# Loading the first 2 MiB of a weight in eight DMAs of 16 strided partitions instead of one of 128

## The chip, the cores and the metric

One core of a Trainium2 chip runs the whole program. The metric is the device time of one execution in microseconds (us). The profile's span of the same execution is about 2 us shorter. The kernel before lay between 139.34 and 139.55 us in six runs.

## The reference

A decode step of a transformer block for 4 tokens, in bf16: layer norm, attention over a window of the last 2048 cached keys, and a gated feed-forward part, with two residual additions.

```python
x = A_x                                                    # [4, 1, 1024]
h  = x + attention(layernorm(x), k_cache, v_cache, wq, wo)   # 32 heads of 128, 4 kv heads
h2 = h + (silu(n @ w1) * (n @ w3)) @ w2                      # n = layernorm(h), F = 3584
```

With 4 tokens there is little arithmetic for each byte. About 55.6 MB of weights and cache have to be read once; wq alone is 8.4 MB.

## The kernel before

All big loads go through one plan. Each takes a 32 KB-a-partition buffer (`stream`, five of them) and is issued on the sync queue, in order, as buffers come free. The first load of wq is cut in two pieces of 2 MiB, so that the q matmuls can begin when the first has landed.

```python
wq_v = A_wq.rearrange("(p i) n -> p (i n)", i=KC)     # 128 partitions, 64 KB each

def load_rows(src, n, r0, pieces):
    t = stream.tile([P, SLOT], BF16, tag="s")
    i = 0
    for m in pieces:
        nc.sync.dma_start(
            out=t[:, i * n : (i + m) * n], in_=src[:, (r0 + i) * n : (r0 + i + m) * n]
        )
        i += m
    return [t[:, k * n : (k + 1) * n] for k in range(i)]
# ... (load_k, load_v alike)
plan = (
    [("wq", load_rows, (wq_v, N_Q, c, [2, 2] if c == 0 else [4])) for c in range(0, KC, RQ)]
    + [("k", load_k, (b,)) for b in range(0, B, BS)]
    # ... v, wo, w1, w3, w2
)
# ...
nc.scalar.dma_start(out=x_sb[:], in_=x_flat)
load_next(5)
# ...
for j in range(JG):          # x once more in another layout; first used after the attention
    nc.scalar.dma_start(
        out=x_q[QD * j : QD * (j + 1) : RS, :], in_=x_flat[:, j * CG : (j + 1) * CG]
    )
# ... layer norm, transposes of x
for kc in range(KC):         # q = x wq, one matmul group for each 1 MiB of wq
    ...
```

Of the kernel before, what the change touches and what calls it, by code (L numbers as in the profile page):

```python
# [10 lines left out]
P = 128  # L11
# [8 lines left out]
def kernel(  # L20
# [13 lines left out]
    nc = tc.nc  # L34

    B, _, D = A_x.shape
    Hkv, Sk, Dh = A_k_cache.shape[1], A_k_cache.shape[2], A_k_cache.shape[3]
    Hq = A_wq.shape[1] // Dh
    REP = Hq // Hkv
    W = min(4096, max(256, Sk // 4))  # L40
    F = B_w1.shape[1]
    KC = D // P
    FC = F // P
    NK = W // P
    NSB = W // 512
    assert B == 4 and D == KC * P and F == FC * P and Hq * Dh == 4096
    assert Dh == P and W == NK * P and B * Hq == P and Hkv == 4
    eps = 1e-5
    qscale = float(Dh) ** -0.5
# [42 lines left out]
    def load_rows(src, n, r0, pieces):  # L92

        t = stream.tile([P, SLOT], BF16, tag="s")
        i = 0
        for m in pieces:
            nc.sync.dma_start(  # L97
                out=t[:, i * n : (i + m) * n], in_=src[:, (r0 + i) * n : (r0 + i + m) * n]
            )
            i += m  # L100
        return [t[:, k * n : (k + 1) * n] for k in range(i)]

# [13 lines left out]
    def load_v(b):  # L116
# [11 lines left out]
    N_Q, N_F = Hq * Dh, F  # L128
# [3 lines that stand above are left out]
        + [("v", load_v, (b,)) for b in range(0, B, BS)]  # L132
        + [("wo", load_rows, (wo_v, D, c, [RO])) for c in range(0, IO, RO)]
        + [("w1", load_rows, (w1_v, N_F, c, [RQ])) for c in range(0, KC, RQ)]
        + [("w3", load_rows, (w3_v, N_F, c, [RQ])) for c in range(0, KC, RQ)]
        + [("w2", load_rows, (w2_v, D, 0, [16])), ("w2", load_rows, (w2_v, D, 16, [5, 4, 2, 1]))]
    )
    loaded = {}
    cursor = [0]
# [19 lines left out]
    for j in range(JG):  # L159
        nc.scalar.dma_start(  # L160
            out=x_q[QD * j : QD * (j + 1) : RS, :], in_=x_flat[:, j * CG : (j + 1) * CG]
# [7 lines left out]
    for c in range(2):  # L169
# [8 lines left out]
        out=xn[:], in0=x_sb[:], scalar1=mv[:, 0:1], scalar2=rstd[:, 0:1],  # L178
# [4 lines left out]
    for kc in range(KC):  # L183
# [15 lines left out]
        out=perm[:].rearrange("p (h dq) -> p h dq", dq=JG),  # L199
        in_=ident[:].rearrange("p (dq h) -> p h dq", dq=JG),  # L200
# [7 lines left out]
    for j in range(2, JG):  # L208
        nc.vector.tensor_tensor(
            out=same[:, 0, :], in0=same[:, 0, :], in1=ident[:, j * QD : (j + 1) * QD], op=ALU.add  # L210
# [24 lines left out]
    for r in range(REP):  # L235
        nc.tensor.transpose(out=qt_ps[:, r, :], in_=q_sb[:, r * Dh : (r + 1) * Dh], identity=ident[:])  # L236
    nc.vector.tensor_copy(
        out=qz[:, :, : Hkv * QD].rearrange("p b (g z) -> p b g z", g=Hkv)[:, :, :, :REP],
        in_=qt_ps[:].rearrange("p r (g x) -> p x g r", g=Hkv)[:, :B, :, :],
# [24 lines left out]
    for u, (b, n) in enumerate(units):  # L264
        k_v = loaded["k"][b].rearrange("p (j d) -> p j d", d=Dh)
        kT = ktpool.tile([P, NJ, P], BF16, tag="kT")
        for t in range(NJ // TB):
            kt_ps = psA.tile([P, TB, P], BF16, tag=f"kt{nt % 4}")
            for jj in range(TB):
                nc.tensor.transpose(  # L270
                    out=kt_ps[:, jj, :], in_=k_v[:, n * NJ + t * TB + jj, :], identity=ident[:]
# [23 lines left out]
        out=Pm[:].rearrange("q (c jq) -> q jq c", jq=NSB), in_=scores_ps[:].rearrange("q (jq c) -> q jq c", jq=NSB),  # L295
# [51 lines left out]
    for i in range(IO):  # L347
# [33 lines left out]
        out=hn[:], in0=h1[:], scalar1=tot[:, 0:1], scalar2=rstd2[:, 0:1],  # L381
# [5 lines left out]
        out=hnT[:].rearrange("p k x -> p (k x)"), in_=hn[:].rearrange("q (c k) -> q k c", k=KC)  # L387
# [5 lines left out]
    def gate_up(kind, out_ps):  # L393
# [27 lines left out]
        out=hgT[:].rearrange("p i x -> p (i x)"),  # L421
        in_=hg[:].rearrange("q s c -> q (s c)").rearrange("q (c i) -> q i c", i=IF),
# [47 lines left out]
```

## Time and profile before

| | before |
|---|---|
| median of 6 runs (lowest to highest) | 139.42 us (139.34 to 139.55) |
| DMA engines busy from, to (profiled run, span 137.4) | 1.77 us, 133.18 us |
| one 16 KB packet of the first 2 MiB, median after the first 16 | 0.611 us |
| first q matmul on wq | 8.20 us |

First come lines of the kernel before's page: the two lines of the 40 slices that concern the DMA engines (busy share in tenths; GB/s moved), the packet count, and the chain of work that ended last, by engine and by line.

```profile
DMA  5999999999999999999999999999999999998950
GB/s 155 444 402 520 391 391 444 420 429 444 405 440 392 421 421 414 423 495 476 401 391 424 453 428 397 459 467 401 409 459 439 426 409 430 448 458 359 420 217 2
DMA packets 4773, 55.74 MB, mean 406 GB/s; under 512 B 376, under 2 KB 408, under 8 KB 2716
...
DMA 70%; PE 19%; ACT 6%; SPq 1%; DVE 1%; issue 1%; ACTq 0%
```

From the second slice to the third last the 16 DMA engines are at 90% or more, but for one slice at 80 to 90%. The kernel is one long load with arithmetic beside it. The chain is 70% DMA.

The windows of the first microseconds of the kernel before follow. The columns are the stretch and its length, busy us (and count) of PE, PEld, DVE, ACT and POOL, the granted TensorE clock, the DMA share and the GB/s. A packet is counted whole in the window in which it starts, so a share can pass 1.

```profile
2.00:4.00 2.00, 0.00 (x0) 0.00 (x0) 1.76 (x5) 0.11 (x1) 0.15 (x1) 1.00 0.77 303
4.00:6.00 2.00, 0.00 (x0) 0.00 (x0) 0.45 (x2) 1.47 (x2) 0.00 (x0) 1.00 0.95 402
6.00:8.00 2.00, 0.65 (x8) 0.65 (x9) 1.44 (x9) 0.00 (x0) 0.00 (x0) 1.00 1.01 428
8.00:10.00 2.00, 1.80 (x16) 0.50 (x16) 0.31 (x3) 0.00 (x0) 0.00 (x0) 1.00 1.07 460
10.00:12.00 2.00, 0.08 (x4) 0.00 (x0) 0.00 (x0) 0.00 (x0) 0.00 (x0) 1.00 1.00 418
12.00:14.00 2.00, 1.05 (x12) 0.38 (x15) 0.00 (x0) 0.00 (x0) 0.00 (x0) 1.00 1.22 524
```

In the windows from 4 us on the stream runs at 400 GB/s and more. The kernel before's timeline (start, length, engine, line, operation) gives the issue of the three wq DMAs, first, on the sync queue:

```profile
0.73 1.33 SPq L97 DMA_DIRECT2D t<-in_A_wq_dram  x3
```

and, on PE, the first matmuls that need them, with the wait just before:

```profile
8.20 1.88 PE L222 MATMUL q_ps<-t,xnT 128*4 128x512 bf16 x16 [1.26 <-DMA t<-in_A_wq_dram]
```

And these are the three long waits of its chain that ended last (start, length, what):

```profile
1.63 20.98 DMA t<-in_A_wq_dram
...
54.23 36.88 DMA t<-in_B_w_dram
...
95.17 37.81 DMA t<-in_B_w_dram
```

The chain goes through a load three times: for wq at the start, and for two stretches of 37 us in the feed-forward part. Between them compute sets buffers free, but the DMA queue has work all that time, so an early loss in the stream reaches the end.

A note on packets. A packet is the piece in which the trace records what a DMA moves: the first 2 MiB stand there as 128 packets of 16 KB, as many as there are partitions with a row of 16 KB. In the trace of before 16 packets are under way at once for 116 of the 137 us. The trace records the start, the length and the size of each packet. It doesn't say which engine or which DMA it was; slices are told apart by the order of their packets, an average over the engines is a sum divided by 16, and numbers "from the packet records" below are counted from these records.

### The profile page before, as it was taken

The numbers are of one execution on the slowest core, as the hardware profiler recorded it, in microseconds if no ns is written. First come the engines' busy times: TensorE is split into PE (matmuls) and PEld (weight loads), VectorE is DVE, ScalarE is ACT, GpSimd is POOL, SyncE is SP. The second block draws the span as 40 slices with busy tenths as digits, with TensorE's granted clock in tenths as the row PEclk, the third lists the DMA queues.
The fourth block names the chain that finished last, engine by engine and source line by source line (L and its number), as shares of the span: only waits on it lengthen the run. The fifth ranks groups of instructions, "written<-read, shape, count | busy, mean of one in ns | idle before, by whom it ended". The sixth has DMA issues, their size and how long they took to land.

```text
span 137.4 us, 2307 instructions
## 1 busy us (share of the span) xinstructions
PE 71.2 (52%) x1045; PEld 45.2 (33%) x1045; DVE 36.3 (26%) x63; ACT 29.0 (21%) x28; POOL 1.6 (1%) x7
## 2 busy tenths in 40 slices
PE   0152304798989889100995579544090530802960
PEld 0110001175656565000894457221030210302830
DVE  6430000244444444601400300530003970160001
ACT  0400000155564646098610000000005000000000
POOL 4000000000000000000000000000000000000000
PEclk9999999999999999975555555558655586555555
DMA  5999999999999999999999999999999999998950
GB/s 155 444 402 520 391 391 444 420 429 444 405 440 392 421 421 414 423 495 476 401 391 424 453 428 397 459 467 401 409 459 439 426 409 430 448 458 359 420 217 2
DMA packets 4773, 55.74 MB, mean 406 GB/s; under 512 B 376, under 2 KB 408, under 8 KB 2716
## 3 DMA queue, kind: packets, MB, share of 16 engines
q1 hardware_dynamic: 4724, 55.58, 95.4%
q8 instruction: 8, 0.13, 0.3%
q10 hardware_dynamic: 40, 0.02, 0.0%
q14 instruction: 1, 0.01, 0.0%
HBM read 55.59 MB, written 0.01 MB: 405 GB/s over the span
## 4 chain that ended last, share of the span: by engine, by line
DMA 70%; PE 19%; ACT 6%; SPq 1%; DVE 1%; issue 1%; ACTq 0%
DMA t<-in_B_w_dram 54%; DMA t<-in_A_wq_dram 15%; PE kt_ps L270 9%; ACT kT L276 5%; PE scores_ps L255 5%; PE q_ps L222 3%; PE g_ps L398 2%; SPq L97 1%; PE y_ps L428 1%; DVE q_sb L232 1%; ACT q_sb L233 0%; DVE res L438 0%; PE qt_ps L236 0%; ACTq L276 0%
## 5 line engine op out<-in xcount | busy, mean ns | idle before, releaser
L276 ACT COPY kT<-kt_ps 128x1024 bf16<-128x1024 bf16 x16 | 15.8, 1014 | 12.0 <-PE kt_ps L270 12.0
L270 PE MATMUL kt_ps<-ident,t 128*128 128x128 bf16 x256 | 16.5, 219 | 0.0
L270 PEld LDWEIGHTS <-t 128*128 128x128 bf16 x256 | 14.4, 98 | 5.0 <-issue 4.9
L274 DVE COPY kT<-kt_ps 128x1024 bf16<-128x1024 bf16 x16 | 11.1, 692 | 15.2 <-PE kt_ps L270 15.2
L398 PEld LDWEIGHTS <-hnT 128*32 128x32 bf16 x128 | 5.5, 140 | 25.0 <-issue 22.7
L222 PE MATMUL q_ps<-t,xnT 128*4 128x512 bf16 x64 | 7.2, 615 | 12.0 <-DMA t<-in_A_wq_dram 12.0
L398 PE MATMUL u_ps<-t,hnT 128*32 128x448 bf16 x64 | 6.4, 576 | 10.6 <-DMA t<-in_B_w_dram 10.6
L255 PE MATMUL scores_ps<-kT,qz 128*32 128x512 bf16 x64 | 9.9, 609 | 3.1 <-ACT kT L276 3.1
L428 PE MATMUL y_ps<-t,hgT 128*32 128x256 bf16 x112 | 6.7, 415 | 7.6 <-DMA t<-in_B_w_dram 7.6
L398 PE MATMUL g_ps<-t,hnT 128*32 128x448 bf16 x64 | 6.3, 574 | 8.0 <-DMA t<-in_B_w_dram 8.0
L322 PE MATMUL OT_ps<-PT_sb,t 128*128 128x8 bf16 x256 | 7.4, 168 | 1.9 <-issue 1.7
L428 PEld LDWEIGHTS <-hgT 128*32 128x32 bf16 x112 | 4.8, 139 | 10.0 <-issue 5.5
L349 PE MATMUL y_ps<-t,o 128*32 128x256 bf16 x128 | 7.2, 418 | 1.7 <-DMA t<-in_A_wo_dram 0.9
L322 PEld LDWEIGHTS <-t 128*128 128x128 bf16 x256 | 7.3, 104 | 2.1 <-issue 2.0
L222 PEld LDWEIGHTS <-xnT 128*4 128x4 bf16 x64 | 2.0, 111 | 16.4 <-issue 16.1
L308 PE MATMUL pt_ps<-Dm,Pm 128*128 128x128 bf16 x16 | 1.9, 308 | 9.3 <-DVE Dm L301 9.3
L349 PEld LDWEIGHTS <-o 128*32 128x32 bf16 x128 | 5.1, 144 | 3.5 <-issue 1.2
L412 DVE RECIPROCAL eg<-eg 128x896 f32<-128x896 f32 x1 | 5.8, 5754 | 0.0
L232 DVE TENSOR_SCALAR q_sb<-q_ps 128x512 bf16<-128x512 f32 x1 | 0.7, 692 | 17.8 <-PE q_ps L222 17.8
L233 ACT ACTIVATE q_sb<-q_ps 128x512 bf16<-128x512 f32 x1 | 0.6, 597 | 21.4 <-DVE q_sb L232 21.4
L308 PEld LDWEIGHTS <-Pm 128*128 128x128 bf16 x16 | 1.6, 142 | 9.8 <-ACT Pm L294 9.8
L294 ACT ACTIVATE Pm<-scores_ps,nmax 128x2048 bf16<-128x2048 f32 x1 | 4.8, 4783 | 0.0
(67 smaller groups left out, 37.0 us busy)
## 6 DMA issues: line engine op xcount, KB each, us to landing
t<-in_B_w_dram SPq DMA_DIRECT2D x4, 3584.0 KB
t<-in_A_k_cache_dram SPq DMA_DIRECT2D x4, 2048.0 KB, 25.6
t<-in_A_v_cache_dram SPq DMA_DIRECT2D x4, 2048.0 KB, 33.0
t<-in_A_wo_dram SPq DMA_DIRECT2D x2, 4096.0 KB, 32.5
t<-in_A_wq_dram SPq DMA_DIRECT2D x2, 2048.0 KB, 9.6
t<-in_A_wq_dram SPq DMA_DIRECT2D x1, 4096.0 KB, 21.0
t<-in_B_w_dram SPq DMA_DIRECT2D x1, 4096.0 KB, 39.9
t<-in_B_w_dram SPq DMA_DIRECT2D x1, 1280.0 KB, 34.9
```

Of the source, the lines that this page charges most:

```text
L222: nc.tensor.matmul(q_ps[QD * g : QD * g + B, hf * 512 : (hf + 1) * 512], lhsT=xnT[:, kc, :], rhs=wq_t[:, c0 : c0 + 512], start=(kc == 0), ...
L255: nc.tensor.matmul(scores_ps[QD * g : QD * (g + 1), n * 512 : (n + 1) * 512], lhsT=qz[:, b, g * QD : (g + 1) * QD], rhs=kT_v[:, g, :, :], ...
L270: nc.tensor.transpose(out=kt_ps[:, jj, :], in_=k_v[:, n * NJ + t * TB + jj, :], identity=ident[:])
L274: nc.vector.tensor_copy(out=kT[:, t * TB : (t + 1) * TB, :], in_=kt_ps[:])
L276: nc.scalar.copy(out=kT[:, t * TB : (t + 1) * TB, :], in_=kt_ps[:])
L294: nc.scalar.activation(out=Pm[:].rearrange("q (c jq) -> q jq c", jq=NSB), in_=scores_ps[:].rearrange("q (jq c) -> q jq c", jq=NSB), func=A ...
L308: nc.tensor.matmul(pt_ps[:, jj, :], lhsT=Pm[:, (jb * JPB + jj) * P : (jb * JPB + jj + 1) * P], rhs=Dm[:], start=True, stop=True)
L322: nc.tensor.matmul(OT_ps[:, b, g * REP : (g + 1) * REP], lhsT=v_t[:, g, j, :], rhs=PT_sb[:, j, g * QD + b * REP : g * QD + (b + 1) * REP], ...
L349: nc.tensor.matmul(y_ps[QD * j : QD * (j + 1), :], lhsT=o4[:, i, :, :].rearrange("p b s -> p (b s)"), rhs=loaded["wo"][i][:, j * CG : (j + ...
L398: nc.tensor.matmul(out_ps[QD * j : QD * (j + 1), hf, :HF], lhsT=hnT[:, k, :], rhs=loaded[kind][k][:, c0 : c0 + HF], start=(k == 0), stop=( ...
L412: nc.vector.reciprocal(out=eg[:], in_=eg[:])
L428: nc.tensor.matmul(y2_ps[QD * j : QD * (j + 1), :], lhsT=hgT[:, i, :], rhs=loaded["w2"][i][:, j * CG : (j + 1) * CG], start=False, stop=(i ...
```

## The change

The intent is to have all 16 DMA engines start at once. With one DMA of 128 partitions the first 16 packets start one after the other over 0.44 us (1.77 to 2.21 us in the trace of before). Each of the eight DMAs of 16 partitions has 16 packets. The rows of one DMA are 8 partitions apart.

```diff
-            nc.sync.dma_start(
-                out=t[:, i * n : (i + m) * n], in_=src[:, (r0 + i) * n : (r0 + i + m) * n]
-            )
+
+            step = 8 if cursor[0] == 0 and i == 0 else 1
+            for p0 in range(step):
+                nc.sync.dma_start(
+                    out=t[p0:P:step, i * n : (i + m) * n],
+                    in_=src[p0:P:step, (r0 + i) * n : (r0 + i + m) * n],
+                )
             i += m
```

An unused constant (`FC`) goes too; that compiles to nothing. Below, one of the eight DMAs is called a slice.

More of the change, by code (lines that the diff above doesn't have):

```diff
@@ L42 @@
     KC = D // P
-    FC = F // P
     NK = W // P
     NSB = W // 512
-    assert B == 4 and D == KC * P and F == FC * P and Hq * Dh == 4096
+    assert B == 4 and D == KC * P and F % P == 0 and Hq * Dh == 4096
     assert Dh == P and W == NK * P and B * Hq == P and Hkv == 4
```

## The prediction

> **What bounds the kernel now.** The loads. The page counts 55.7 MB at a mean of 406 GB/s, and its line of DMA shares is at 9 (90% or more) in nearly every slice. Windows of 2 us show no gap: the 16 DMA engines are busy from 1.63 us, when the first packet of wq starts, to about 133 us; a tail of 4 us follows. The chain that ended last is 70% DMA; PE is busy 52% of the span. When the first w1 load is issued at 54.2 us, 33.5 MB had been asked for and about 22 MB delivered (estimate from the windows), so the queue doesn't run dry. The time is start of the stream + its service time + tail; what the change does to the stream moves the end one for one.
>
> **The start now.** The first DMA of 2 MiB is issued at 0.73 us (0.4 us). Its first 16 packets, 16 KB each, start between 1.63 and 2.1 us and end at 2.7 to 3.2 us, however early they started. After that a 16 KB packet takes 0.61 us on every engine (packet records of the trace). The last of 8 per engine ends at 7.5 us; the first q matmul starts at 8.20 us.
>
> **What the change does.**
> 1. It removes the stagger of the first packets: 0.1 to 0.3 us less, as their ends hardly depend on their starts.
> 2. It adds seven issues of about 0.4 us, 2.9 us on the sync queue. An issue is shorter than a packet (0.61 us), so the engines stay fed. Some later issues will wait for reused semaphores; none should starve the engines. Seven more completion packets of 9 ns per engine: 0.1 us.
> 3. It changes which partitions are written together. [...] No run here shows this yet.
> So I expect a 16 KB packet of these DMAs to take about 1.2 us instead of 0.61: 8 x 0.6 = +4.9 us on the stream.
>
> **Sum.** -0.2 + 0.1 + 4.9 = +4.8 us, nearly all on the critical path: 144.2 us; I say 144.0. [...] Range 139.1 to 144.8. Chances: faster by over 2%: 0.01; within 2%: 0.29; slower by over 2%: 0.70.
>
> **What would show it.** Right: between 2 and 12 us the windows' GB/s fall to about 210 while the DMA share stays near 1; the packets take 1.2 us; the first q matmul starts at about 13 us; everything later is shifted by nearly 5 us, its stages unchanged. Wrong: packets stay at 0.61 us and the first matmul starts at about 8 us.
>
> **What would make it wrong.** [...] Or an issue costs more than 0.6 us and starves the engines: then gaps show between 2 and 8 us.

The 1.2 us, twice the measured 0.61 us, was the assumption. The three terms of the sum, -0.2, +0.1 and +4.9, come to +4.8 us, and 139.4 + 4.8 is 144.2 us. The outcome without the long packets: the first two terms alone, 139.3 us or a little less.

What 1 and 2 rest on is in the packet records of before: the first packet to start (1.77 us) ends at 3.00 us, the last of the first 16 to start (2.21 us) at 3.02 us, and a completion packet has a median length of 9 ns.

The times that it takes from the packet records (1.63, 2.7 to 3.2, 7.5 us) are counted from an origin about 0.13 us late. On the profile's axis the first packet starts at 1.77 us and the last of the first 2 MiB ends at 7.65 us. The differences that it sums are not touched by this.

## The result, and the profile after

| | before | after |
|---|---|---|
| median of 6 runs (lowest to highest) | 139.42 us (139.34 to 139.55) | 145.0 us (144.16 to 145.88) |
| ratio, 95% interval | | 1.040 (1.0345 to 1.0456) |
| first packet starts | 1.77 us | 2.14 us |
| one 16 KB packet of the first 2 MiB, median after the first 16 | 0.611 us | 1.220 us |
| last packet of the first 2 MiB ends | 7.65 us | 12.10 us |
| last big packet ends | 133.18 us | 137.94 us |

A ratio is the mean time of one kernel's fast runs over that of the other's fast runs of the same rounds, so it is not quite the ratio of the medians. The trace of after is of its fastest run (144.16 us, span 142.2). The six runs scatter over 1.7 us, those of before over 0.2.

The same lines of after's page:

```profile
DMA  5998999999999999999999999999999999998950
GB/s 141 224 221 300 447 443 433 396 420 443 438 438 391 416 421 422 416 423 527 443 406 410 424 408 459 408 444 436 411 444 432 420 436 486 415 424 365 424 229 2
DMA packets 4885, 55.74 MB, mean 392 GB/s; under 512 B 488, under 2 KB 520, under 8 KB 2828
...
DMA 69%; PE 19%; ACT 5%; ACTq 2%; SPq 1%; issue 1%; DVE 1%
```

The second to fourth slice fell to between 221 and 300 GB/s while the busy share stayed at 8 to 9. From there on the lines look as they did. There are 112 packets more, the completion packets of seven more DMAs (16 each).

The same windows of the kernel after:

```profile
2.00:4.00 2.00, 0.00 (x0) 0.00 (x0) 1.76 (x5) 0.00 (x0) 0.15 (x1) 1.00 1.13 279
4.00:6.00 2.00, 0.00 (x0) 0.00 (x0) 0.24 (x2) 1.58 (x2) 0.00 (x0) 1.00 1.11 231
6.00:8.00 2.00, 0.64 (x8) 0.56 (x8) 1.48 (x8) 0.00 (x0) 0.00 (x0) 1.00 1.03 232
8.00:10.00 2.00, 0.00 (x0) 0.00 (x0) 0.47 (x4) 0.00 (x0) 0.00 (x0) 1.00 0.81 180
10.00:12.00 2.00, 0.00 (x0) 0.00 (x0) 0.00 (x0) 0.00 (x0) 0.00 (x0) 1.00 1.10 246
12.00:14.00 2.00, 0.79 (x8) 0.27 (x12) 0.00 (x0) 0.00 (x0) 0.00 (x0) 1.00 0.88 360
```

About 230 GB/s with the engines busy. They work nearly all the time and move half as much. The window from 8 to 10 us is emptier (0.81): by the packet records only 9 of 16 engines have a packet under way at 9.1 us, between the sixth and the seventh slice.

The issue of the ten wq DMAs, in the timeline of after's sync queue:

```profile
0.73 9.34 SPq L99 DMA_DIRECT2D t<-in_A_wq_dram  x10
```

The first matmuls on wq, in its timeline of PE:

```profile
13.21 1.88 PE L225 MATMUL q_ps<-t,xnT 128*4 128x512 bf16 x16 [6.07 <-DMA t<-in_A_wq_dram]
```

And the three long waits of its chain that ended last, with two pieces just before the first of them:

```profile
2.82 5.62 DMA x_q<-in_A_x_dram
8.45 0.53 SPq L99
...
9.66 18.04 DMA t<-in_A_wq_dram
...
59.45 36.34 DMA t<-in_B_w_dram
...
99.89 37.84 DMA t<-in_B_w_dram
```

The first matmul on wq comes 5.0 us later (13.21 against 8.20). The two late waits for the feed-forward weights begin 5.2 and 4.7 us later, and they are as long as before (36.34 and 36.88, 37.84 and 37.81 us). So nearly all of the loss is made in the first 12 us and carried to the end. New in the chain is an x_q load of 2 KB, 5.62 us long, after which an issue of wq follows. Before, the chain began with the wq issues themselves.

The ten wq issues took the sync queue 9.34 us instead of 1.33 for three. Its own waits in the first 16 us show why (who, for what, us in total, times, longest). In the kernel before no wq issue waits; the three longest waits are of the k and v loads:

```profile
SPq L121 <- PE kt_ps L270: 27.2, 1, 27.2
SPq L109 <- DMA t<-in_A_wq_dram: 5.2, 1, 5.2
SPq L121 <- DMA t<-in_A_wq_dram: 1.7, 1, 1.7
```

After the change wq's own issues (L99) wait:

```profile
SPq L99 <- DMA x_q<-in_A_x_dram: 2.3, 2, 1.7
SPq L99 <- DMA t<-in_A_wq_dram: 1.3, 1, 1.3
```

In the records of the issues each DMA names a semaphore by which it tells that it has landed, called its completion semaphore here. The program has eight of them (100, 102 to 106, 108, 110) and reuses them in turn; an issue that reuses one waits for it. In the trace of after the fourth slice and those after it reuse one. The fifth, for one, has the semaphore of the first slice, whose 16 signals come from 3.67 to 4.53 us, and is issued at 4.55 us, 1.3 us after the issue of the fourth ended. Three of the slices have semaphores of the tiny x_q loads (2 KB each). These are not needed until after the attention, but here a slice isn't issued before they land: the seventh waits 1.7 us, until 7.84 us. What it costs, e8 shows.

### The profile page after: what moved, and what is told of

Read it like the earlier page. It is cut to its first block, busy times and chain, and to the rows that moved or that the text cites. A ratio compares the mean times of both kernels' runs of the same rounds, so it can differ in the third digit from the quotient of the medians.

```text
span 142.2 us, 2317 instructions
## 1 busy us (share of the span) xinstructions
PE 68.9 (48%) x1045; PEld 43.6 (31%) x1045; DVE 36.3 (26%) x63; ACT 29.0 (20%) x28; POOL 1.6 (1%) x7
## 4 chain that ended last, share of the span: by engine, by line
DMA 69%; PE 19%; ACT 5%; ACTq 2%; SPq 1%; issue 1%; DVE 1%
DMA t<-in_B_w_dram 52%; DMA t<-in_A_wq_dram 13%; PE kt_ps L273 8%; ACT kT L279 5%; PE scores_ps L258 5%; DMA x_q<-in_A_x_dram 4%; PE q_ps L225 3%; PE g_ps L401 2%; SPq L99 1%; ACTq L163 1%; PE y_ps L431 1%; DVE q_sb L235 0%; ACT q_sb L236 0%; ACTq L152 0%; DVE res L441 0%
## 5 line engine op out<-in xcount | busy, mean ns | idle before, releaser
L431 PE MATMUL y_ps<-t,hgT 128*32 128x256 bf16 x112 | 5.8, 371 | 8.7 <-DMA t<-in_B_w_dram 8.7
L431 PEld LDWEIGHTS <-hgT 128*32 128x32 bf16 x112 | 4.3, 128 | 10.6 <-issue 6.3
L352 PE MATMUL y_ps<-t,o 128*32 128x256 bf16 x128 | 6.4, 394 | 0.8 <-DVE o L341 0.8
```

The costliest lines, as they stand in the source:

```text
L352: nc.tensor.matmul(y_ps[QD * j : QD * (j + 1), :], lhsT=o4[:, i, :, :].rearrange("p b s -> p (b s)"), rhs=loaded["wo"][i][:, j * CG : (j + ...
L431: nc.tensor.matmul(y2_ps[QD * j : QD * (j + 1), :], lhsT=hgT[:, i, :], rhs=loaded["w2"][i][:, j * CG : (j + 1) * CG], start=False, stop=(i ...
```

## The experiments

There were twelve experiments, in four groups on one chip each, every group with the kernel before beside it (139.38 to 139.45 us in the median). SBUF is the on-chip memory whose 128 partitions the loads fill. Theory A says that what counts is which partitions a slice writes: that packets to some sets of them take longer. In some expectations, times and packet lengths that stand without a name are theory A's (for e12 see there). Its rivals are that reads 512 KB apart are slow (the pitch), and that small DMAs cost by their number.

| run | first 2 MiB as | median us (range) | ratio | packet, median |
|---|---|---|---|---|
| e1 | the change again | 144.92 (144.22 to 145.62) | 1.041 | 1.18 |
| e7 | the change's partitions, neighbouring HBM rows | 145.53 (144.45 to 146.16) | 1.043 | 1.22 |
| e3 | 8 x 16 neighbouring partitions | 151.19 (150.51 to 151.5) | 1.083 | 2.13 |
| e6 | 8 x 16 partitions, step 4, halves | 144.52 (143.93 to 145.76) | 1.037 | 1.12 |
| e4 | the change's slices, alternating | 143.62 (143.39 to 144.92), three fast runs | 1.033 | 1.05 |
| e12 | 4 x 32 partitions, step 4 | 140.5 (140.31 to 140.84) | 1.007 | 0.61 |
| e2 | 8 x 128 partitions of 2 KB | 142.0 (141.22 to 142.08) | 1.018 | (2 KB) |
| e9 | e2 with x_q moved | 141.52 (141.38 to 141.6) | 1.015 | (2 KB) |
| e5 | the change (x_q not really moved) | 145.64 (144.18 to 145.96) | 1.043 | 1.25 |
| e8 | the change with x_q moved | 143.92 (143.75 to 144.0) | 1.032 | 1.27 |
| e11 | e8 again | 143.91 (143.86 to 144.13) | 1.033 | 1.27 |
| e10 | the kernel before with x_q moved | 139.15 (138.97 to 139.22) | 0.998 | 0.62 |

The last column is the median length of a 16 KB packet of the first 2 MiB, without the first 16, in us.

### e1: the change again

The edit: none.

> The changed kernel itself, again. Its six runs fell into two groups, 144.2 to 144.3 us and 145.7 to 145.9 us, and only one of the first group left a trace. All theories expect the two groups again. Theory 'late slice' (the seventh slice's issue waits for the semaphore of an x_q load, which lands late behind long wq packets): in a trace of the second group the gap of the DMA engines between the sixth and the seventh slice is about 1.5 us longer than in the first trace (0.5 us there). Rival[...]: in the second group the 16 KB packets of the first 2 MiB take longer, with a mean near 1.4 us instead of 1.2, and no longer gap.

144.22 to 145.62 us, four runs. The "two groups" were an accident of six runs, since 144.57 and 145.28 lie between them. So what is there is a scatter of 1.7 us. The traced run (144.57) is of neither group, so the two theories were not tested as stated; its packets took 1.18 us, not the 1.4 of the rival. See "The scatter" below.

### e7: same partitions, other rows

```diff
-                    out=t[p0:P:step, ...], in_=src[p0:P:step, ...],
+                    out=t[q:P:8, ...], in_=src[16 * q : 16 * q + 16, ...],
```

A small copy permutes x to match, so the result is right.

> The changed kernel writes the same partitions (p0, p0+8, ...) in each of the eight DMAs, but reads 16 neighbouring rows of wq for them (64 KB apart instead of 512 KB), with x permuted to match, so the result stays right. [...] as the changed kernel, 144.0 to 146 us, packets of about 1.2 us. Rival 'HBM pitch' (reads 512 KB apart are slow): packets of about 0.61 us, 139.4 to 140.2 us.

145.53 us, packets of 1.22 us. The pitch of the reads is out: with rows 64 KB apart the slices are as slow as with 512 KB. What e7 keeps from the change is where the slices write.

### e3: 16 neighbouring partitions

```diff
-            for p0 in range(step):                 # step = 8 for the first piece
-                nc.sync.dma_start(out=t[p0:P:step, ...], in_=src[p0:P:step, ...])
+            for a in range(8):                     # first piece only
+                nc.sync.dma_start(out=t[16*a : 16*a+16, ...], in_=src[16*a : 16*a+16, ...])
```

> Eight DMAs of 16 neighbouring partitions each[...]. [...] packets of the first 2 MiB take about 2.4 us, the stream is 8 x 1.8 = 14.6 us longer than before: 153 to 155 us. Rival (any DMA of 16 partitions costs the same, however they lie): 144 to 146 us, packets of 1.2 us.

151.19 us, packets of 2.13 us. Three windows of e3:

```profile
6.00:8.00 2.00, 0.65 (x8) 0.57 (x8) 1.43 (x9) 0.00 (x0) 0.00 (x0) 1.00 0.90 108
8.00:10.00 2.00, 0.00 (x0) 0.00 (x0) 0.32 (x3) 0.00 (x0) 0.00 (x0) 1.00 0.90 108
10.00:12.00 2.00, 0.00 (x0) 0.00 (x0) 0.00 (x0) 0.00 (x0) 0.00 (x0) 1.00 0.96 115
```

The engines are 90% busy or more and move 108 to 115 GB/s, half of what the change moved. So the length of a packet goes with the set of partitions that a DMA writes: 0.61 us for all 128 (before), 1.22 for 16 with a step of 8 (after), 2.13 for 16 neighbours. That is shorter than the 2.4 us expected, and the time fell below the expected range. The 2.4 us, about four times the 0.61, was the assumption. From the third slice on the 16 packets of a slice start over 1.35 to 1.7 us, so two slices overlap for much of the time. Whether that is why the packets are shorter than expected, no run tests.

e3 and e7 read the same rows of wq in the same order and differ only in the partitions to which the rows go (and in the copy of x). Packets of 2.13 us against 1.22: so it is the writes.

One more reading. The first packet of e3 starts at 1.76 us, as before the change. With a step of 4 or 8 it starts at 2.09 to 2.16 us in every run. The records of the single issues show the same: the first took 0.38 us before, 0.39 us in e3, and 0.62 to 0.64 us in slices of 16 with a step of 4 or 8. So the change delays the start that it was to hasten. The longer issue is 0.23 of the 0.37 us (0.62 against 0.38); the rest is not explained.

### e6: other sets of 16 partitions

```diff
-            for p0 in range(step):
-                nc.sync.dma_start(out=t[p0:P:step, ...], in_=src[p0:P:step, ...])
+            for h in range(2):
+                for a in range(4):
+                    rows = slice(64*h + a, 64*h + 64, 4)
+                    nc.sync.dma_start(out=t[rows, ...], in_=src[rows, ...])
```

> Eight DMAs of 16 partitions with a step of 4, four in the lower and four in the upper half of the partitions. [...] the rows in HBM are 256 KB apart instead of 512. [...] packets of 1.1 to 1.3 us, 143.5 to 146 us, as the change. Rival (the step of 8 or the 512 KB matters): packets near 0.61 us, 139.5 to 141 us.

144.52 us, median packet 1.12 us: within what theory A expected, and far from its rival. Neither the step of 8 nor the pitch is needed.

### e4: another order

```diff
-            for p0 in range(8):
+            for p0 in (0, 4, 1, 5, 2, 6, 3, 7):
```

> The same eight DMAs as in the change in another order: first partitions 0, 4, 1, 5, 2, 6, 3, 7[...]. [...] the packets take between 0.61 and 1.2 us, 0.8 to 1.1 in the mean, and the time falls to 141.5 to 143.7 us. Rival (a cost for each DMA of 16 partitions, or of the pitch): no change from the changed kernel, 144.2 to 146 us.

Packets of 1.05 us, within the range expected, and shorter than with the change's order: the order of the slices alone moves their length, which a fixed cost for each DMA can't do. The median of the three fast runs, 143.62 us, is inside the expected range (141.5 to 143.7), but one of the three, 144.92, is not. A fourth run, 145.9 us, is listed as slow, being over 1.5% above the fastest; its clock (0.782) is no lower than that of the others, so it may be the scatter. Half confirmed.

The change's own trace shows something like it once. In e4 the change's first four slices (those that begin at partitions 0 to 3) alternate with its last four (4 to 7). In the change's order a slice of the one four follows one of the other only at the fifth. The packets of the fifth slice, which overlap with the fourth, take about 1.1 us in after and in e8, those of the slices around it 1.22 to 1.28. Why the order counts, no run shows.

### e12: 32 partitions in one DMA

```diff
-            step = 8 if cursor[0] == 0 and i == 0 else 1
+            step = 4 if cursor[0] == 0 and i == 0 else 1
```

> Four DMAs of 32 partitions (step 4)[...]. If what counts is [...], packets are near 0.61 us and the time 139.5 to 141 us. If what counts is [...], packets are 1.0 to 1.3 us and the time 143 to 146 us.

140.5 us and packets of 0.61 us: the first of the two outcomes. Three windows of e12:

```profile
4.00:6.00 2.00, 0.00 (x0) 0.00 (x0) 0.27 (x2) 1.58 (x2) 0.00 (x0) 1.00 1.03 378
6.00:8.00 2.00, 0.66 (x8) 0.58 (x8) 1.47 (x8) 0.00 (x0) 0.00 (x0) 1.00 0.96 346
8.00:10.00 2.00, 0.71 (x8) 0.32 (x12) 0.46 (x4) 0.00 (x0) 0.00 (x0) 1.00 0.93 387
```

346 to 387 GB/s, against 180 to 232 in the same windows after the change. This is the nearest thing to the change that lacks the long packets: strided partitions, four small DMAs, a late start (2.09 us), issues that wait for x_q. It costs 1.06 us over before, 0.32 of it the late start. So the long packets are most of the 5.6 us (e12 has four DMAs, the change eight, so they are not the whole difference). The second outcome is out. Why packets to 32 partitions with a step of 4 took 0.61 us and to 16 with a step of 8 took 1.22, no run shows.

### e2: eight DMAs, all 128 partitions

```diff
-            for p0 in range(step):
-                nc.sync.dma_start(out=t[p0:P:step, ...], in_=src[p0:P:step, ...])
+            for c in range(8):                     # an eighth of the piece's columns
+                cols = slice(i*n + c*wd, i*n + (c+1)*wd)
+                nc.sync.dma_start(out=t[:, cols], in_=src[:, cols])      # r0 = 0 here
```

> The same 2 MiB in eight DMAs too, but each of 128 partitions and an eighth of the columns (2 KB a partition): same number of DMAs, same bytes[...]. [...] nearly the time before, plus what 2 KB packets cost: 64 packets of 84 ns instead of 8 of 611 ns on each engine is +0.5 us, and some tenths for a later start: 139.7 to 140.5 us. Rival 'eight small DMAs cost by their number' (issue, semaphores): 143 us or more, with gaps between the slices.

142.0 us: neither. The first range, theory A's, was too low and the rival's too high. From the packet records, 1.3 us of the 2.6 is longer packet time (2 KB packets), the rest idle engines. (The 84 ns of the expectation is the median 2 KB packet in the trace of before.)

### e9: e2 with the x_q loads moved

```diff
-        nc.scalar.dma_start(out=x_q[...], in_=x_flat[...])     # at the start
+        nc.sync.dma_start(out=x_q[...], in_=x_flat[...])       # behind the first wo load
```

> Eight DMAs of 128 partitions x 2 KB, as in e2 (142.0 us), with the x_q loads moved as in e8. In e2 the packets' time accounts for 1.3 us of the 2.6 us, idle engines between the DMAs for about 1.3 us, and there the later issues waited for reused semaphores. Theory 'semaphore wait': the gaps go, and 140.3 to 140.9 us remain. Rival 'fixed cost of each small DMA on the engines': the gaps stay, 141.5 to 142.2 us.

141.52 us: the rival's side, if only by a little. Here the slices were issued every 0.45 to 0.48 us, but for one gap of 0.82, without a long wait, but they finish 0.7 to 1.2 us apart, and between 3.5 and 7 us only 9 to 16 of the 16 engines are busy. So in this run small DMAs cost something by their number, even well fed: 2.1 us over the kernel before (141.52 against 139.45), longer packet time included. What holds them up is open. In the change this cost probably doesn't add, as a slice takes 1.2 us on the engines there and they are busy; that is argued, not shown.

### e5: a run that did not do what it said

```diff
-    for j in range(JG):          # in the beginning
-        nc.scalar.dma_start(out=x_q[...], in_=x_flat[...])
     # ... layer norm, q, scores, attention
+    for j in range(JG):          # the same loads on the same (ACT) queue
+        nc.scalar.dma_start(out=x_q[...], in_=x_flat[...])
```

> The changed kernel with the four x_q loads put off until after the attention, so that no slice of wq can wait for their semaphores. Theory 'late slice': no gap between the slices, one group of times only, 143.6 to 144.2 us, with less than 0.4 us between the fastest and the slowest run. Rival[...]: two groups 1.5 us apart, as before. [...] the packets of the first 2 MiB still take about 1.2 us either way.

The scheduler put the loads where they had been, at 1.34 us, since nothing holds them back. So e5 is one more repeat of the change: 144.18 to 145.96 us.

### e8: the change with the x_q loads moved, and e11, the same once more

```diff
-    nc.scalar.dma_start(out=x_q[...], in_=x_flat[...])     # in the beginning
+    nc.sync.dma_start(out=x_q[...], in_=x_flat[...])       # behind the first wo load
```

> The run e5 did not do what it said: its x_q loads were still issued at 1.3 us, because the loads of the ACT queue have nothing to wait for, so it was one more repeat. Here the four x_q loads go on the sync queue behind the first wo load, so no slice shares a reused semaphore with them. Theory 'semaphore wait': the waits of the sixth to ninth wq issues for x_q (up to 1.7 us) are gone, the slices are issued about every 0.5 us, and the idle gaps of the engines between slices shrink; the fastest run gains 0.2 to 0.5 us (143.7 to 144.1 us). If the spread of 1.9 us between runs also came from these waits, all runs lie within 0.4 us; rival: the spread stays, because it comes from one DMA engine that begins the next 128-partition load late (by 1.6 us in one trace), whatever x_q does. Packets stay at about 1.2 us.

> The kernel of e8 once more, on whatever chip comes: its four runs lay within 0.25 us, where ten runs of the changed kernel spread over 1.7 us. If taking x_q out of the way of the slices is what removed the spread, all runs lie again within 0.4 us, at 143.6 to 144.2 us, and in the trace no DMA engine is more than 0.5 us behind the middle one at the end of the load that follows the slices. If e8 was luck, runs at 144.9 us or above turn up.

All nine runs lie between 143.75 and 144.13 us. The scatter is gone. It is not the chip: e4 ran on the same one, and even its fast runs lie 1.5 us apart. The sync queue's waits of e8:

```profile
SPq L112 <- DMA t<-in_A_wq_dram: 2.1, 4, 0.7
SPq L124 <- DMA t<-in_A_wq_dram: 1.5, 2, 0.8
```

No slice of wq waits any more. The k and v loads wait a little for slices, while the last 6 MiB of wq are still queued (they land at 27 us). The packets are still 1.27 us long. The engines now have no gap between slices, and yet the first 2 MiB end at 12.33 us, no sooner than in the trace of after (12.10), as the packets are a little longer. So the wait itself cost the fastest run of the change nothing that shows here, though the chain ran through it; what x_q costs is the scatter. With the scatter gone, what is left is +4.5 us over the kernel before (143.92 against 139.45).

### e10: the kernel before with the x_q loads moved

```diff
-    nc.scalar.dma_start(out=x_q[...], in_=x_flat[...])     # in the beginning
+    nc.sync.dma_start(out=x_q[...], in_=x_flat[...])       # behind the first wo load
```

> Control for e8: the kernel before, with the x_q loads moved to the sync queue behind the first wo load, and nothing else. If e8 gained because its slices no longer wait for x_q, the move alone is worth nothing here, where no early load is starved by such a wait: 139.3 to 139.5 us. If the move itself is worth what e8 gained over the middle of the changed kernel's runs (1 us), this falls to about 138.4 us.

139.15 us, ratio 0.998 (0.9963 to 0.9988). The move alone is worth about 0.3 us here, just below the range that I gave, and far from 1 us. Only about 0.1 of it is in the profile's span (137.2 to 137.4 us in its five runs, 137.3 to 137.6 in the nine of before), the rest outside. So of the 1.1 us between the medians of after and e8 about 0.3 may be the move as such and 0.8 is the scatter. It is also the only version here that is faster than both kernels, by a quarter of a per cent.

### The scatter

A DMA of wq or k has 16 completion packets in the packet records, as many as there are engines. I take them to be one from each; the records don't name the engine. How far the last of them is behind the middle one then tells how far the slowest engine lags. Here it is at the load that follows the slices (the second 2 MiB of wq), and four loads later, at the third load of k:

```
run (profiled)      time us         lag of the slowest engine, us
                                    2nd wq load   3rd k load
before              139.4           0.26          1.35
e8, e11             144.0, 144.1    0.30, 0.19    1.61, 1.67
after               144.16          0.73          1.37
e5                  144.18          0.15          1.46
e1                  144.57          1.79          1.82
e4                  144.92          1.45          1.99
e6                  145.76          1.31          2.61
e7                  145.79          2.19          2.21
```

In e1 the lag stays at 1.79 to 1.82 us over these loads, so an engine that is late there stays late. In the trace of e7 one engine stands idle for about 1.6 us between its last slice and its next packet (found by linking each packet to the one that ended just before it). Later, eight 16 KB packets of the instruction queue take an engine's time too (0.88 to 0.97 us each in the traces of before and after; the page of e8 lists eight as well). In e6 the lag of the slowest goes from 1.31 to 2.61 us just after one of them (at 37.6 us), in e5 from 0.15 to 1.45 us (at 36.0 us), in before from 0.26 to 1.35. I take it that it depends on which engines they meet. So the first column alone does not give the time; the second goes with it for the runs of the changed kernels that keep x_q, but for the order of the last two. These are single traces. Which engine a packet took isn't recorded, so this is read from the times alone.

That the x_q loads in the way of the slices bring the scatter about is shown by e8 and e11, nine runs: their spans are 142.0 to 142.3 us, where the three best runs of after lie (142.2, 142.3, 142.2), and the other three of after, at 143.7 and 143.8, have no counterpart. e2 and e9 agree (a range of 0.86 us, and 0.22 with x_q moved). Whether it is the wait of the issue or the x_q packets themselves on the engines was not told apart, and why an engine with issued work stands idle is open.

## Why the prediction was right or wrong

**Right: the direction and the main term.** A packet of the strided slices took twice as long as before: predicted 1.2 us, measured 1.22. The shift carried to the end one for one, with the later stages unchanged in length, as the two long waits show. By e3 and e7 it is the writes: the same rows of wq in the same order took 2.13 us a packet to 16 neighbouring partitions and 1.22 us to 16 with a step of 8. By the runs the set of partitions counts, and not only their number or the step: 16 with a step of 4 took 1.12 us (e6), 32 with a step of 4 took 0.61 (e12), as all 128 do. Why, no run shows.

**The sum, term by term**, for the fastest run (the trace of after), from the packet records, for an engine on average:

| term | predicted | measured |
|---|---|---|
| start of the first packet (stagger) | -0.2 | +0.37 (1.77 to 2.14) |
| packets of the first 2 MiB | +4.9 | +3.75 (5.48 to 9.23) |
| packets of the rest, mostly those right after the slices | 0 | +0.40 (125.43 to 125.83) |
| completion packets | +0.1 | +0.12 |
| unequal engines, gaps, other queues | 0 | +0.12 |
| last packet ends later | +4.8 | +4.76 (133.18 to 137.94) |

That the sum was right for this run is luck: the errors cancel. The packet term was oversized: the first 16 packets took a median of 1.17 us already before (a slow first packet), and they did not get longer (0.98 us in after). The start term had the wrong sign: the first three issues with strided partitions took 0.57 to 0.62 us, where the contiguous wq loads before took 0.38 to 0.43 (e3 against the others shows the same), and the first packet came 0.37 us later.

**Wrong: step 2, "Some later issues will wait for reused semaphores; none should starve the engines."** I saw that semaphores are reused and did not ask whose landing the slices would wait for. It was that of the x_q loads, on the other queue, and the slices waited up to 1.7 us. Engines did run dry: 7 of 16 at 9.1 us even in the fastest run (nine packets under way). There it cost nothing that shows, but in other runs an engine fell 1.3 to 2.2 us behind (e1, e4, e6, e7: 144.57 to 145.79 us). This put the median at 145.0 us, above the range (144.8). With x_q out of the way, the kernel takes 143.75 to 144.13 us in all nine runs (e8, e11), where the prediction said 144.0. A part of that, about 0.3 us, is the move itself (e10), so the close hit is luck in part. How the x_q loads make one engine late is open. The same step had the issue too short: 0.57 to 0.62 us in e8 where it said 0.4. That stayed hidden because the packets took 1.2 us.

**Wrong: the range.** It left 0.8 us above the point, where the changed kernel's own six runs lie 1.7 us apart (those of before 0.2). The waits at the start made the engines unequal here (a lag of 1.79 us in e1, of 0.30 in e8), and the mean service time then tells too little.

**The other ways to be wrong.** An issue costing more than 0.6 us happened at the start (0.62 us for the first), without starving the engines.

## What to carry to other kernels

When you cut a DMA by partitions, measure the length of a packet for the set of partitions that each piece writes: here 16 with a step of 8 took 1.22 us a 16 KB packet, 16 with a step of 4 within a half 1.12, and 16 neighbours 2.13, where all 128, or 32 with a step of 4, took 0.61. A busy DMA share with half the GB/s (here about 230 where before had over 400) is the sign. Ask too which earlier load each new DMA's completion semaphore belongs to: here a 2 KB load that nobody needs yet held up a slice for 1.7 us, and with these loads in the way the runs scattered over 1.7 us instead of 0.2. And in this stream-bound kernel a slowest DMA engine that was 1.3 to 2.2 us behind at the second wq load (e1, e4, e6, e7) went with times of 144.6 to 145.8 us, against 144.0 to 144.2 us where it was 0.15 to 0.73 us behind (e8, e11, after, e5), so look at how far apart they end, not only at their mean. A chain that runs through a wait does not prove that the wait costs time: take the wait away, as e8 did, and see.
